# Query features halved in rows and turned by a transposing DMA

## The chip, the cores and the metric

The kernel runs on one core of a Trainium2 chip. The metric is the device time of one execution in microseconds; the time before is the median of three runs. A profiled execution has a time of its own, and a span, which runs from its first instruction to its last. TensorE is PE in the profile, VectorE DVE, ScalarE ACT, GpSimd POOL and SyncE SP; SP only issues DMAs here.

## The reference

Two independent attention blocks with 2048 tokens, 1024 features and 32 heads of 32 are computed, and their outputs stand side by side. Part A is an attention over four segments with a memory, and its output projection is the last stage of the kernel. The change is in part B:

```python
def _B_ref(x, wqkv, w_phi, wo):
    qkv = (x @ wqkv).reshape(B, S, 3, H, Dh).transpose(2, 0, 3, 1, 4)
    q, k, v = qkv[0], qkv[1], qkv[2]
    pq = einsum("bhsd,hdf->bhsf", q, w_phi)
    pk = einsum("bhsd,hdf->bhsf", k, w_phi)
    phi_q = concatenate([softmax(pq), softmax(-pq)], axis=-1)
    phi_k = concatenate([softmax(pk), softmax(-pk)], axis=-1)
    kv = einsum("bhsf,bhsd->bhfd", phi_k, v)
    z  = einsum("bhsf->bhf", phi_k)
    num = einsum("bhqf,bhfd->bhqd", phi_q, kv)
    den = einsum("bhqf,bhf->bhq", phi_q, z)[..., None] + 1e-6
    return (num / den).transpose(0, 2, 1, 3).reshape(B, S, D) @ wo
```

## The kernel before

**Numbers in two halves.** Almost every large product is done in float16, with each operand split in two float16 halves, "hi" and "lo" (lo is what hi leaves over). A product is then three matmuls: hi·hi, hi·lo and lo·hi. Making the two halves is called halving here: ACT writes hi as a copy, DVE writes lo as a subtraction.

**Stages.** Part A comes first, then the keys and values of part B, then the stage of this change, B's queries, then A's output projection. The query stage runs over 16 blocks of 128 tokens in pairs. For a pair, one Strassen product (`strassen`, L560 on: seven products of 12 matmuls of 512 columns, L584) makes the projected queries with the tokens in the rows: four tiles of 128 tokens by 512 features, that is for two blocks times two halves `hb` of 16 heads. It reads its left operand from slots that SP loads with seven DMAs of 256 KB a pair (`xkept`, L572). Each tile goes through `expo` (L1225 to L1251): two reductions and two subtractions on DVE, Exp on ACT (L1245), a sum on DVE (L1248). This gives `e`, 128 tokens by 16 heads by 2 signs by 32, float32, and `r`, the reciprocals of the softmax sums.

**The work around the change** is done for each tile (32 in all):

- POOL multiplies `e` by the key sums (L1550, two pieces), DVE sums it to `dn` (L1553, two pieces) and works out the common denominator (L1556 to L1560); L1561 multiplies it into `r`; POOL multiplies `e` by `r` (L1563). `e` is then the normalised features, 128 tokens in the rows, 1024 values each.
- TensorE turns `e` in eight float32 transposes of 128x128 (L1569) into two PSUM banks named `s`, four to a bank.
- ACT and DVE halve what stands in the banks into `pt` (L1571, L1573), with the scale 2^14, 512 values a row at a time. `pt` has the features in the rows and the tokens in the columns.
- 24 matmuls (L1582) multiply `pt` by the halved key-value sums `kls` into a bank `pv`; ACT and DVE halve that into `ot` (L1586, L1588).

When both tiles of a block are through, `project` (L1458) multiplies `ot` by the output weights (24 matmuls at L370 for each half of the columns) and SP stores the result (L1465).

**What sets the order.** The kernel is a graph of operations. Each `op(engine, duration, function, r=..., w=..., prio=...)` states what it reads and writes and a modelled duration, and a list scheduler walks the graph once by modelled times and priorities. The order in which it emits operations is the fixed order of each engine's instructions; on the chip an engine waits at its next instruction until that instruction's data are there. `lat` is the modelled time from the issue of a DMA to its landing, `kb` its size, and `port=True` marks a DVE operation on SBUF alone that the planner keeps apart from POOL's work. Buffers rotate under a tag: `e` has five slots, `pt` three, `ot` four, `os` one. An operation that writes a slot waits until the last reader of its previous contents is done.

Of the kernel before, what the change touches and what calls it, by code (L numbers as in the profile page):

```python
# [78 lines left out]
class Graph:  # L79
# [35 lines left out]
    def op(self, eng, dur, fn, r=(), w=(), prio=0, lat=0.0, short=False, port=False, need=(), kb=256):  # L115
        o = Op()
        o.short, o.port = short, port or eng == "POOL"
        o.eng, o.dur, o.fn, o.prio, o.lat, o.kb = eng, dur, fn, (prio, len(self.ops)), lat, kb
        o.banks = []
        ends, starts = set(), set()  # L120
        for b in need:
            if b.prev[0] is not None:
                ends.update(b.prev[0].ops)
        for write, accs in ((0, r), (1, w)):
            for acc in accs:
                b, key = acc if isinstance(acc, tuple) else (acc, None)
                old, last, opened = b.prev
                if old is not None:
                    ends.update(old.ops)
                if not b.ops and last is not None:  # L130
                    starts.add(last.ops[0])
                if opened is not None:
                    starts.add(opened)
                for k in (list(b.writer) if key is None else [key, None]):
                    if k in b.writer:
                        ends.add(b.writer[k])
                if write:
                    for k in (list(b.readers) if key is None else [key, None]):
# [12 lines left out]
        self.ops.append(o)  # L151
        return o
# [99 lines left out]
SP, PE, ACT, DVE, POOL = "SP", "PE", "ACT", "DVE", "POOL"  # L252
# [3 lines left out]
def tile_kernel(ctx: ExitStack, tc: tile.TileContext, ax, aw, awv, awo, beta, bx, bwqk, bwv, bphi, bwo, out):  # L256
    nc = tc.nc
# [29 lines left out]
    ident = const.tile([128, 128], F32, name="ident")  # L287
# [39 lines left out]
    for t in vfb:  # L327
        nc.gpsimd.memset(t[:, :, 128:132], 1.0)

    G = Graph(pools)  # L330
    op = G.op
# [5 lines left out]
       w=[gates], prio=0.2, lat=2.0, kb=16)  # L337
# [12 lines left out]
    def bank(tag, shape, line=None):  # L350
        b = G.bank(tag, shape, F32, line or tag)
        psums.add(b)
        return b
# [272 lines left out]
    for t in stk:  # L626
        op(ACT, 2.0, lambda t=t: nc.scalar.activation(t()[96:104, 1], sel[96:104, :, None].to_broadcast([8, 4, 512]), AF.Copy),
           w=[(t, (1, 3))], prio=0.3)
# [625 lines left out]
    def bc32(r):  # L1254
        return r()[:, :, :, None].to_broadcast([128, 16, 2, 32])

    def pairs(e):
        return e().rearrange("p (a two) s d -> p a (two s d)", two=2)

# [82 lines left out]
    for at_, p in enumerate(SEQ):  # L1342
        P = PB + 2 * at_
# [15 lines left out]
        for i in range(2):  # L1359
            if p in VT:  # L1360
                n = 2 * VT.index(p) + i
# [52 lines left out]
    P = PB + NT  # L1414
# [102 lines left out]
    for c in range(NT):  # L1517
        P = Q0 + c
        if c % 2 == 0:
            sk, er = times(c // 2, 0, P - 1.2), {}  # L1520

            def qout(i, hb, ps, er=er, sk=sk, P=P):
                er[i, hb] = expo(ps, P, sk)

            strassen(x, wqf, P - 1.2, ("proj", "proj", "proj"), CS, qout)
            if c + 2 < NT:
                x = x1 if c == 0 else xkept(c // 2 + 1, XS, P)
        ot = G.buf("b", [128, 2112], F16, "ot", 4)
        if c == 2:
            for f, i in (("B11", 8), ("B21", 13), ("T1", 12)):  # L1530
                wform[f] = G.buf("slot", [128, 2, 4, 512], F16, f"S{i}")
        if c in (1, 2, 3, 4):
            sizes_out(c - 1, P + 0.5)
        if c in (5, 7, 9, 11):
            weights((c - 5) // 2, P + 0.5)
        if c == 14:
            for i, f in enumerate(SECOND):
                wform[f] = G.buf("slot", [128, 2, 4, 512], F16, f"S{i}")
                op(SP, 0.6, lambda i=i, f=f: nc.sync.dma_start(wform[f](), wo_d[i]), r=[(wob, i)],
                   w=[(wform[f], (a, n)) for a in range(2) for n in range(4)], prio=P + 0.5, lat=1.0, kb=1024)  # L1540

        def otv(ot=ot):
            return ot()[:, 0:2048].rearrange("p (a g t) -> p a g t", a=2, g=NG)

        for hb in range(2):
            e, r = er[c % 2, hb]
            dn = G.buf("b", [128, 16, 2], F32, "dn", 2)
            for a in range(2):
                h0 = 16 * hb + 8 * a
                op(POOL, 1.35, lambda a=a, h0=h0, e=e: nc.gpsimd.tensor_tensor(  # L1550
                    e()[:, 8 * a:8 * a + 8], e()[:, 8 * a:8 * a + 8], zv()[:, h0:h0 + 8], op=OP.mult),
                   r=[zb, r], w=[(e, ("x", a))], prio=P)
                op(DVE, 0.66, lambda a=a, e=e, dn=dn: nc.vector.tensor_reduce(  # L1553
                    dn()[:, 8 * a:8 * a + 8], e()[:, 8 * a:8 * a + 8], axis=AX.X, op=OP.add), r=[(e, ("x", a))], w=[(dn, a)], prio=P)
            d1 = G.buf("b", [128, 16], F32, "d1", 2)
            op(DVE, 0.1, lambda dn=dn, r=r: nc.vector.tensor_tensor(dn(), dn(), r(), op=OP.mult),  # L1556
               r=[dn, r], w=[dn], prio=P)
            op(DVE, 0.1, lambda dn=dn, d1=d1: nc.vector.scalar_tensor_tensor(
                d1(), dn()[:, :, 0], 1e-6, dn()[:, :, 1], op0=OP.add, op1=OP.add), r=[dn], w=[d1], prio=P)
            op(DVE, 0.15, lambda d1=d1: nc.vector.reciprocal(d1(), d1()), r=[d1], w=[d1], prio=P)  # L1560
            op(DVE, 0.1, lambda d1=d1, r=r: nc.vector.tensor_tensor(  # L1561
                r(), r(), d1()[:, :, None].to_broadcast([128, 16, 2]), op=OP.mult), r=[d1, r], w=[r], prio=P)
            op(POOL, 1.95, lambda e=e, r=r: nc.gpsimd.tensor_tensor(e(), e(), bc32(r), op=OP.mult),  # L1563
               r=[e, r], w=[e], prio=P)
            pt = G.buf("b", [128, 2, 8, 128], F16, "pt", 3)
            for q in range(2):
                ps = bank("s", [128, 4, 128])
                for i in range(4):
                    op(PE, 0.11, lambda q=q, i=i, e=e, ps=ps: nc.tensor.transpose(  # L1569
                        ps()[:, i, :], pairs(e)[:, 4 * q + i, :], ident), r=[e], w=[ps], prio=P)  # L1570
                op(ACT, 0.55, lambda q=q, pt=pt, ps=ps: nc.scalar.activation(pt()[:, 0, 4 * q:4 * q + 4], ps(), AF.Copy, scale=2.0 ** 14),  # L1571
                   r=[ps], w=[(pt, (0, q))], prio=P)
                op(DVE, 0.62, lambda q=q, pt=pt, ps=ps: nc.vector.scalar_tensor_tensor(  # L1573
                    pt()[:, 1, 4 * q:4 * q + 4], ps(), 2.0 ** 14, pt()[:, 0, 4 * q:4 * q + 4], op0=OP.mult, op1=OP.subtract),
                   r=[ps, (pt, (0, q))], w=[(pt, (1, q))], prio=P)
            pn = bank("pv", [128, 4, 128])

            def f(pn=pn, pt=pt, hb=hb):
                for g in range(4):
                    for a, b in ((0, 0), (0, 1), (1, 0)):  # L1580
                        for k in range(2):
                            nc.tensor.matmul(pn()[64 * k:64 * k + 64, g, :], kls()[:, a, 8 * hb + 2 * g + k, :], pt()[:, b, 2 * g + k, :],  # L1582
                                             start=(a + b == 0), stop=(a == 1), skip_group_check=True)

            op(PE, 0.85, f, r=[(kls, (0, hb)), (kls, (1, hb)), pt], w=[pn], prio=P)
            op(ACT, 0.55, lambda pn=pn, hb=hb, otv=otv: nc.scalar.activation(  # L1586
                otv()[:, 0, 4 * hb:4 * hb + 4, :], pn(), AF.Copy, scale=2.0 ** -15), r=[pn], w=[(ot, (0, hb))], prio=P)
            op(DVE, 0.62, lambda pn=pn, hb=hb, otv=otv: nc.vector.scalar_tensor_tensor(  # L1588
                otv()[:, 1, 4 * hb:4 * hb + 4, :], pn(), 2.0 ** -15, otv()[:, 0, 4 * hb:4 * hb + 4, :], op0=OP.mult, op1=OP.subtract),
               r=[pn, (ot, (0, hb))], w=[(ot, (1, hb))], prio=P)  # L1590
        project(lambda a, g: (ot, None, lambda otv=otv: otv()[:, a, g, :]), bo, c * 128, 1024, P + 1.1)
# [116 lines left out]
```

## Time and profile before

| | |
|---|---|
| runs before, median of 3 (lowest to highest) | 1734.23 us (1733.72 to 1735.37) |
| profiled execution, its time | 1733.96 us |
| profiled execution, its span | 1732.3 us |
| granted TensorE clock, mean | 0.996 |
| ACT busy, share of the span | 1157.8 us, 67% |
| POOL busy, share of the span | 939.5 us, 54% |

The span leaves out what the profiled time has beside it, 1.7 us. A row of groups gives the line, the engine, the operation, output and inputs by name, rows by elements and type, and how often; then the busy time with the mean of one, and the idle time just ahead of them with what ended it. In a row of the timeline the first number is the start, the second the duration, and what stands in brackets is the idle time before and what ended it. A row "x24" there sums 24 instructions.

### The profile page before, as it was taken

Reading aid. Unit: us, or ns where it says so; the run is one execution under the profiler, and the core shown is the slowest. Engines: PE = TensorE matmul, PEld = TensorE weight load, DVE = VectorE, ACT = ScalarE, POOL = GpSimd, SP = SyncE. Lnnn points to the kernel's source line nnn. Section 1 sums busy time; section 2 is a strip of 40 time slices with the busy share of each in tenths; the row PEclk is TensorE's granted clock in tenths of the full one; section 3 lists DMA queues with packets and bytes.
Section 4 is the critical chain, followed back from the end, with each engine's and each line's share of the span. In section 5 each row is a group of like instructions: output and inputs, shape, how many; then the busy total and the mean of one; then the engine's idle time right before and its main releaser. Section 6 shows DMA issues by size and latency. Waiting matters only on the chain.

```text
span 1732.3 us, 39104 instructions
## 1 busy us (share of the span) xinstructions
PE 1697.2 (98%) x14664; PEld 1030.3 (59%) x14664; DVE 1384.0 (80%) x3269; ACT 1157.8 (67%) x2131; POOL 939.5 (54%) x1184
## 2 busy tenths in 40 slices
PE   8999999999999999999999999999999999999999
PEld 6667666767776676776754444444545555554444
DVE  6889899999997787889874988877978877786541
ACT  8788889888888798677772676765545544444331
POOL 3346477754478866656651777645737675440000
PEclk9999999999999999999999999999999999999999
DMA  6556455775666664743467474567413332234311
GB/s 210 160 166 185 151 169 174 223 209 169 224 181 185 188 165 122 227 162 106 136 179 262 131 240 130 180 211 251 161 44 118 103 111 85 63 139 146 122 66 63
DMA packets 194141, 273.62 MB, mean 158 GB/s; under 512 B 72224, under 2 KB 125216, under 8 KB 187424
## 3 DMA queue, kind: packets, MB, share of 16 engines
q1 hardware_dynamic: 193952, 271.13, 49.5%
q8 instruction: 115, 1.88, 0.4%
q14 instruction: 74, 0.61, 0.1%
HBM read 160.12 MB, written 85.00 MB: 142 GB/s over the span
## 4 chain that ended last, share of the span: by engine, by line
PE 40%; DVE 11%; ACT 2%; POOL 1%; issue 1%; POOLq 0%; ACTq 0%; DVEq 0%
PE proj L584 14%; PE misc L370 7%; PE proj L1636 5%; PE s L1636 2%; PE proj L370 2%; PE s L584 2%; DVE mx L1238 2%; PE misc L1636 1%; DVE r L1248 1%; PE pv L1582 1%; PE misc L584 1%; PE s L1569 1%; DVE e L1240 1%; DVE dn L1553 1%; DVE e L1242 1%; DVE pt L1389 1%
## 5 line engine op out<-in xcount | busy, mean ns | idle before, releaser
L370 PE MATMUL proj<-S,S 128*128 128x128 f16 (+1 forms) x3072 | 507.1, 300 | 4.3 <-DVE S L405 1.9
L370 PEld LDWEIGHTS <-S 128*128 128x128 f16 x4608 | 328.7, 98 | 151.2 <-issue 10.8
L584 PE MATMUL proj<-S,S 128*128 128x512 f16 x1584 | 360.6, 379 | 2.4 <-ACT cs L590 2.4
L584 PEld LDWEIGHTS <-S 128*128 128x128 f16 x2016 | 192.7, 98 | 221.7 <-issue 3.3
L960 POOL TENSOR_SCALAR_AFFINE_SELECT ph<-ph 128x256 f16<-128x256 f16 (+1 forms) x448 | 191.6, 450 | 172.5 <-DVE ph L954 133.7
L852 DVE CUSTOM_DVE_ANT_0 s<-s,causal 128x512 f32<-128x512 f32 (+3 forms) x512 | 242.6, 510 | 10.3 <-PE s L846 7.0
L954 DVE SCALAR_TENSOR_TENSOR ph<-s,ph 128x512 f16<-128x512 f32 x320 | 209.6, 683 | 51.5 <-ACT ph L953 49.3
L953 ACT ACTIVATE ph<-s 128x512 f16<-128x512 f32 x320 | 190.2, 659 | 0.3
L370 PE MATMUL misc<-S,ot 128*128 128x512 f16 x768 | 174.9, 380 | 0.0
L1245 ACT ACTIVATE e<-e,sk 128x256 f32<-128x256 f32 x256 | 113.4, 498 | 65.5 <-DVE e L1242 60.8
L370 PEld LDWEIGHTS <-ot 128*128 128x128 f16 x768 | 73.4, 98 | 81.8 <-issue 0.9
L846 PE MATMUL s<-S 96*128 96x512 f16 (+3 forms) x512 | 113.9, 299 | 2.2 <-DVE ph L954 1.6
L947 PE MATMUL s<-S 104*128 104x512 f16 (+3 forms) x512 | 113.1, 299 | 2.2 <-DVE ph L954 1.5
L951 ACT ACTIVATE s<-s,os 128x512 f32<-128x512 f32 x160 | 106.2, 717 | 6.9 <-PE s L947 5.3
L1550 POOL TENSOR_TENSOR e<-e,zb 128x512 f32<-128x512 f32 x64 | 80.2, 1277 | 55.7 <-DVE r L1248 35.1
L951 ACT ACTIVATE s<-s,bd 128x512 f32<-128x512 f32 x160 | 105.4, 705 | 6.5 <-PE s L947 6.4
L370 PE MATMUL proj<-wv,S 128*128 128x128 f16 x1536 | 101.8, 219 | 0.0
L983 PEld LDWEIGHTS <-ph 128*128 128x128 f16 x2560 | 87.3, 96 | 18.1 <-issue 2.2
L983 PE MATMUL pv<-vl,ph 128*128 128x66 f16 (+1 forms) x2560 | 91.9, 184 | 2.0 <-DVE oall L987 1.0
L1248 DVE TENSOR_REDUCE r<-e 128x32 f32<-128x1024 f32 x64 | 77.1, 1206 | 16.2 <-ACT e L1245 16.2
L1563 POOL TENSOR_TENSOR e<-e,r 128x1024 f32<-128x1024 f32 x32 | 61.9, 1938 | 34.5 <-DVE r L1561 27.5
L852 DVE DVE_READ_ACCUMULATOR2_ANT mt<- 128x1 f32 x512 | 72.6, 142 | 0.0
(344 smaller groups left out, 3344.1 us busy)
## 6 DMA issues: line engine op xcount, KB each, us to landing
S<-xf_d SPq DMA_DIRECT2D x126, 256.0 KB
S<-h SPq DMA_DIRECT2D x192, 128.0 KB
S<-wf_d SPq DMA_DIRECT2D x21, 1024.0 KB
st<-bwqk SPq DMA_DIRECT2D x64, 256.0 KB
out<-os SPq DMA_DIRECT2D x40, 256.0 KB
S<-aw SPq DMA_DIRECT2D x16, 512.0 KB
wa_d<-S SPq DMA_DIRECT2D x16, 512.0 KB
wf_d<-fo SPq DMA_DIRECT2D x32, 256.0 KB
```

The costliest lines, as they stand in the source:

```text
L370: op(PE, dur, lambda c=c, a=a, b=b, lv=lv, rv=rv: nc.tensor.matmul(pv(), lv(), rv(), start=(c == 0 and a + b == 0), stop=(c == n - 1 and a ...
L584: op(PE, 0.215, lambda n=n, a=a, b=b, lv=lv, rv=rv: nc.tensor.matmul(ps(), lv(), rv(), start=(start and n == 0 and a + b == 0), stop=(n == ...
L846: nc.tensor.matmul(ps()[:, o:o + 128 * i + 128], st()[0:96, 0, h, 128 * i:128 * i + 128], st()[0:96, 1, h, 0:128 * i + 128], start=True, s ...
L852: dve(0.12 + 0.00113 * n, lambda h=h, i=i, o=o, n=n: nc.vector.tensor_tensor_reduce(ps()[:, o:o + n], ps()[:, o:o + n], causal[:, 512 - n: ...
L947: nc.tensor.matmul(ps()[:, o:o + n], st()[0:104, 1, h, 128 * j:128 * j + 128], st()[0:104, 0, h, 128 * j:512], start=True, stop=True)
L951: act(0.59, lambda: nc.scalar.activation(ps(), ps(), AF.Exp, bias=0.0, scale=bdv()[:, 3, i2, 0:1]), r=[(bd, i2)], w=[ps])
L953: act(0.5, lambda: nc.scalar.activation(ph()[:, 0], ps(), AF.Copy, scale=2.0 ** 14), r=[ps], w=[(ph, 0)])
L954: dve(0.6, lambda: nc.vector.scalar_tensor_tensor(ph()[:, 1], ps(), 2.0 ** 14, ph()[:, 0], op0=OP.mult, op1=OP.subtract), r=[ps, (ph, 0)], ...
L960: nc.gpsimd.affine_select(pd, pd, pattern=[[0, n], [1, 128]], compare_op=OP.is_ge, fill=0.0, base=0, channel_multiplier=-1)
L983: nc.tensor.matmul(ps()[:, i, n0:n1], ph()[:, a, o:o + 128], vl()[:, j, h, n0:n1], start=(i == 0 and a == 0), stop=(j == min(i, 2)), skip_ ...
L1245: op(ACT, 0.41, lambda i=i: nc.scalar.activation(e()[:, 4 * i:4 * i + 4], e()[:, 4 * i:4 * i + 4], AF.Exp, bias=0.0, scale=sk()[:, i:i + 1 ...
L1636: op(PE, 0.215, lambda n=n, a=a, b=b: nc.tensor.matmul(ps(), v(a)[:, n, :], wform[w]()[:, b, n, :], start=(start and n == 0 and a + b == 0 ...
```

## The change

The normalised features are halved while the tokens are still in the rows, and the halves are turned by one DMA for each tile.

- The factor 2^14 moves from the halving into the multiplication of `r` (L1564 in the new numbering; below the helper `ev` all lines move down by 3, and after the edit by 7).
- For each tile a second buffer `eh` is taken from the same five slots as `e`. Read as float16 it holds 128 rows of 2 x 1024: all hi halves, then all lo halves.
- ACT writes hi (L1575) and DVE lo (L1577), 512 values a row at a time, from `e` in SBUF; before, both read PSUM.
- SP issues one transposing DMA (L1580), 128 x 2048 float16 in, `pt` as 128 x 16 x 128 out, 512 KB. The planner counts 0.6 us of issue and 2.0 us to the landing.
- The eight transposes on TensorE and their use of the banks `s` are gone. The 24 matmuls of the tile (now L1589) and what follows are unchanged.

```diff
+    def ev(e):
+        return e().rearrange("p h s d -> p (h s d)")
...
-            op(DVE, 0.1, lambda d1=d1, r=r: nc.vector.tensor_tensor(
-                r(), r(), d1()[:, :, None].to_broadcast([128, 16, 2]), op=OP.mult), ...)
+            op(DVE, 0.1, lambda d1=d1, r=r: nc.vector.scalar_tensor_tensor(
+                r(), r(), 2.0 ** 14, d1()[:, :, None].to_broadcast([128, 16, 2]), op0=OP.mult, op1=OP.mult), ...)
             op(POOL, 1.95, lambda e=e, r=r: nc.gpsimd.tensor_tensor(e(), e(), bc32(r), op=OP.mult),
                r=[e, r], w=[e], prio=P)
             pt = G.buf("b", [128, 2, 8, 128], F16, "pt", 3)
+            eh = G.buf("b", [128, 16, 2, 32], F32, "e", 5)
+
+            def hv(eh=eh):
+                return eh().rearrange("p h s d -> p (h s d)").bitcast(F16).rearrange("p (a n) -> p a n", a=2)
+
             for q in range(2):
-                ps = bank("s", [128, 4, 128])
-                for i in range(4):
-                    op(PE, 0.11, lambda ...: nc.tensor.transpose(
-                        ps()[:, i, :], pairs(e)[:, 4 * q + i, :], ident), r=[e], w=[ps], prio=P)
-                op(ACT, 0.55, lambda ...: nc.scalar.activation(pt()[:, 0, 4 * q:4 * q + 4], ps(), AF.Copy, scale=2.0 ** 14), ...)
-                op(DVE, 0.62, lambda ...: nc.vector.scalar_tensor_tensor(
-                    pt()[:, 1, 4 * q:4 * q + 4], ps(), 2.0 ** 14, pt()[:, 0, 4 * q:4 * q + 4], op0=OP.mult, op1=OP.subtract), ...)
+                op(ACT, 0.53, lambda ...: nc.scalar.activation(
+                    hv()[:, 0, 512 * q:512 * q + 512], ev(e)[:, 512 * q:512 * q + 512], AF.Copy), r=[e], w=[(eh, (0, q))], prio=P)
+                op(DVE, 0.7, lambda ...: nc.vector.tensor_tensor(
+                    hv()[:, 1, 512 * q:512 * q + 512], ev(e)[:, 512 * q:512 * q + 512], hv()[:, 0, 512 * q:512 * q + 512], op=OP.subtract),
+                   r=[e, (eh, (0, q))], w=[(eh, (1, q))], prio=P, port=True)
+            op(SP, 0.6, lambda pt=pt, hv=hv: nc.sync.dma_start_transpose(
+                pt().rearrange("p a g t -> p (a g) t"), hv().rearrange("p a n -> p (a n)")),
+               r=[(eh, (a, q)) for a in range(2) for q in range(2)], w=[pt], prio=P, lat=2.0, kb=512)
```

**The order on TensorE.** Late in the query stage, before the change, a pair's Strassen product ends (L584, `proj`), 12 transposes follow (one and a half tiles), and the next four stand three matmuls further on in the projection of an earlier block (L370, `misc`, left operand `ot`):

```order
L584 LDWEIGHTS S_14955
L584 MATMUL proj<-S_19188,S_14955 128x512
L1569 MATMUL s<-ident,e 128x128 x12
L370 LDWEIGHTS ot
L370 MATMUL misc<-S_19610,ot 128x512
L370 LDWEIGHTS ot
L370 MATMUL misc<-S_19610,ot 128x512
L370 LDWEIGHTS ot
L370 MATMUL misc<-S_19610,ot 128x512
L1569 MATMUL s<-ident,e 128x128 x4
```

After the change a product that has begun (S_13978 is one of its seven left operands) is interrupted by the first tile's matmuls, which read `pt` as the DMA left it:

```order
L584 LDWEIGHTS S_13978
L584 MATMUL proj<-S_18784,S_13978 128x512
L584 LDWEIGHTS S_13978
L584 MATMUL proj<-S_18784,S_13978 128x512
L1589 LDWEIGHTS kls
L1589 MATMUL pv<-pt,kls 64x128
L1589 LDWEIGHTS kls
L1589 MATMUL pv<-pt,kls 64x128
```

The transposes are gone, and 24 matmuls that wait for a DMA now stand inside a product, with the rest of the product and the projections behind them.

**The order on DVE,** after the change, from right behind the two pieces of a first tile's halving (L1577) to the result of its matmuls (L1595); the pieces of L1577 shown here are the second tile's:

```order
L1556 TENSOR_REDUCE dn<-e 128x16 x2
L1559 TENSOR_TENSOR dn<-dn,r 128x32
L1577 TENSOR_TENSOR e<-e 128x512 x2
L1556 TENSOR_REDUCE dn<-e 128x16
L1559 TENSOR_TENSOR dn<-dn,r 128x32
L1561 SCALAR_TENSOR_TENSOR d_22411<-dn 128x16
L1561 SCALAR_TENSOR_TENSOR d_22413<-dn 128x16
L1563 RECIPROCAL d_22411<-d_22411 128x16
L1563 RECIPROCAL d_22413<-d_22413 128x16
L1564 SCALAR_TENSOR_TENSOR r<-r,d_22411 128x32
L1564 SCALAR_TENSOR_TENSOR r<-r,d_22413 128x32
L1595 SCALAR_TENSOR_TENSOR ot<-pv,ot 128x512
```

This is all that DVE has between a tile's halving and the result that comes back through DMA, TensorE and ACT; the other two tiles' halvings stand behind L1595.

**The order on SP,** for one pair. Before, stores of the output (`os`, one slot) and loads of the next left operands follow one another:

```order
L1465 DMA out<-os 128x512 x4
L572 DMA S_13978<-xf_d 128x1024 x4
L572 DMA S_14955<-xf_d 128x1024 x3
L1465 DMA out<-os 128x512 x4
```

After, the four transposing DMAs of the pair stand between them:

```order
L1468 DMA out<-os 128x512 x2
L1580 DMA_TRANSPOSE pt<-e 128x16x128
L1468 DMA out<-os 128x512
L1580 DMA_TRANSPOSE pt<-e 128x16x128
L1468 DMA out<-os 128x512
L572 DMA S_13978<-xf_d 128x1024 x2
L1580 DMA_TRANSPOSE pt<-e 128x16x128
L572 DMA S_13978<-xf_d 128x1024
L1580 DMA_TRANSPOSE pt<-e 128x16x128
L572 DMA S_13978<-xf_d 128x1024
L572 DMA S_14955<-xf_d 128x1024 x3
```

Loads of the next product now stand behind transpositions in one queue, and a transposition waits at its place until its `eh` is written and its `pt` is free.

More of the change, by code (lines that the diff above doesn't have):

```diff
@@ L1560, in tile_kernel @@
             op(DVE, 0.15, lambda d1=d1: nc.vector.reciprocal(d1(), d1()), r=[d1], w=[d1], prio=P)
-            op(DVE, 0.1, lambda d1=d1, r=r: nc.vector.tensor_tensor(
-                r(), r(), d1()[:, :, None].to_broadcast([128, 16, 2]), op=OP.mult), r=[d1, r], w=[r], prio=P)
+            op(DVE, 0.1, lambda d1=d1, r=r: nc.vector.scalar_tensor_tensor(
+                r(), r(), 2.0 ** 14, d1()[:, :, None].to_broadcast([128, 16, 2]), op0=OP.mult, op1=OP.mult), r=[d1, r], w=[r], prio=P)
             op(POOL, 1.95, lambda e=e, r=r: nc.gpsimd.tensor_tensor(e(), e(), bc32(r), op=OP.mult),
@@ L1565, in tile_kernel @@
             pt = G.buf("b", [128, 2, 8, 128], F16, "pt", 3)
+            eh = G.buf("b", [128, 16, 2, 32], F32, "e", 5)
+            def hv(eh=eh):
+                return eh().rearrange("p h s d -> p (h s d)").bitcast(F16).rearrange("p (a n) -> p a n", a=2)
             for q in range(2):
-                ps = bank("s", [128, 4, 128])
-                for i in range(4):
-                    op(PE, 0.11, lambda q=q, i=i, e=e, ps=ps: nc.tensor.transpose(
-                        ps()[:, i, :], pairs(e)[:, 4 * q + i, :], ident), r=[e], w=[ps], prio=P)
[L1571 to L1575, printed above, removed]
+                op(ACT, 0.53, lambda q=q, e=e, hv=hv: nc.scalar.activation(
+                    hv()[:, 0, 512 * q:512 * q + 512], ev(e)[:, 512 * q:512 * q + 512], AF.Copy), r=[e], w=[(eh, (0, q))], prio=P)
+                op(DVE, 0.7, lambda q=q, e=e, hv=hv: nc.vector.tensor_tensor(
+                    hv()[:, 1, 512 * q:512 * q + 512], ev(e)[:, 512 * q:512 * q + 512], hv()[:, 0, 512 * q:512 * q + 512], op=OP.subtract),
[3 more added lines that the diff above has]
+               r=[(eh, (a, q)) for a in range(2) for q in range(2)], w=[pt], prio=P, lat=2.0, kb=512)
             pn = bank("pv", [128, 4, 128])
```

## The prediction

> **What bounds the kernel now.** I read the page's first lines, then windows over the stage that the change touches, then what TensorE waits for there.
>
> ```profile
> span 1732.3 us, 39104 instructions
> PE 1697.2 (98%) x14664; PEld 1030.3 (59%) x14664; DVE 1384.0 (80%) x3269; ACT 1157.8 (67%) x2131; POOL 939.5 (54%) x1184
> ...
> 1223.00:1265.00 42.00, 36.57 (x267) 20.46 (x264) 41.86 (x77) 20.43 (x43) 28.44 (x22) 0.96 0.36 137
> ...
> 1223.00:1583.00 360.00, 353.49 (x2397) 183.81 (x2394) 293.31 (x523) 167.18 (x323) 197.00 (x145) 1.00 0.32 108
> ...
> 1419.70:1466.10 46.40, 46.33 (x310) 23.86 (x309) 36.32 (x63) 20.40 (x41) 29.78 (x23) 1.00 0.28 86
> 1466.10:1512.40 46.30, 46.30 (x312) 23.85 (x310) 34.92 (x63) 17.73 (x36) 17.55 (x12) 1.00 0.21 63
> ...
> 1520.00:1570.00 50.00, 49.35 (x372) 26.50 (x370) 44.44 (x81) 26.02 (x50) 18.39 (x12) 1.00 0.43 155
> ```
>
> A window's columns are its length, then busy PE, weight loads, DVE, ACT, POOL, then the granted clock, the DMA share and GB/s. The query stage runs from 1223 to 1583 us. In it PE is busy 353.5 of 360 us at full clock and DVE 293.3. The two rows from 1419.7 are one pair of token blocks each: 46.3 us with PE never idle and DVE at 35 to 36. Only the head of the stage (DVE 41.86 of 42.00) and its end (DVE 44.4 of 50) are near DVE's limit. So TensorE sets the pace, and work taken from it in the steady pairs shortens the kernel for as long as the rest keeps up. Its waits in the stage say the same:
>
> ```profile
> PE pv L1582 <- DVE kls L1445: 4.0, 1, 4.0
> PE misc L1419 <- DVE za L1405: 1.3, 1, 1.3
> PE s L1569 <- POOL e L1563: 1.1, 2, 0.7
> ```
>
> **Removed from TensorE.** 32 tiles lose eight float32 transposes each.
>
> ```profile
> L1569 PE MATMUL s<-ident,e 128*128 128x128 f32 x256 | 33.6, 274 | 1.1 <-POOL e L1563 1.1
> L1571 ACT ACTIVATE pt<-s 128x512 f16<-128x512 f32 x64 | 34.6, 592 | 29.4 <-PE s L1569 29.4
> L1573 DVE SCALAR_TENSOR_TENSOR pt<-s,pt 128x512 f16<-128x512 f32 x64 | 41.0, 680 | 3.0 <-ACT pt L1571 2.8
> L1386 ACT ACTIVATE pt<-e 128x512 f16<-128x512 f32 x64 | 37.5, 620 | 27.6 <-PE kv L1396 14.3 <-POOL e L1354 12.9 <-POOL pt L1389 0.4
> L1389 DVE TENSOR_TENSOR pt<-e,pt 128x512 f16<-128x512 f32 x32 | 29.9, 948 | 4.5 <-ACT pt L1386 4.4
> L1553 DVE TENSOR_REDUCE dn<-e 128x16 f32<-128x512 f32 x64 | 42.5, 671 | 3.9 <-POOL e L1550 3.8
> ```
>
> 33.6 us busy, about 34 with the waits they stood behind, 4.2 a pair: a pair of 46.3 becomes 42.1 on TensorE. This is the most that can be won.
>
> **Exchanged on ACT and DVE.** The halving keeps its 64 + 64 instructions but reads SBUF. The nearest rows are the same two operations on the key features: ACT 620 against 592 ns, which is nothing on an engine busy 18 to 20 us of 46. On DVE the mean is 948 against 680, because POOL works beside it; undisturbed it would be the old 680. I take 948: 0.27 x 8 = 2.1 us a pair, so DVE is busy about 37.7 us (35.6 + 2.1). The factor 2^14 rides in a multiplication on 128x32 that is there in either kernel: nothing.
>
> **Added: the transposing DMA.** The trace has none. It moves 512 KB from SBUF to SBUF, and the result is wanted by the 24 matmuls of L1582. Call the time from the issue to its landing D.
>
> ```profile
> 789.45 0.55 SPq L1042 DMA_DIRECT2D wf_d<-fo  x1
> 792.63 0.63 ACT L482 ACTIVATE fo<-quad 128x512 f16<-128x512 f32 x1 [2.40 <-DMA wf_d<-fo]
> ...
> 585.83 0.51 SPq L1042 DMA_DIRECT2D wf_d<-fo  x1
> 592.94 0.63 ACT L482 ACTIVATE fo<-quad 128x512 f16<-128x512 f32 x1 [6.08 <-DMA wf_d<-fo]
> ...
> 1545.04 0.32 SPq L1601 DMA_DIRECT2D e<-oa_d  x1
> 1548.95 0.72 ACT L403 ACTIVATE h<-e,osc 128x512 f16<-128x512 f32 x1 [2.49 <-DMA e<-oa_d]
> ...
> DMA packets 194141, 273.62 MB, mean 158 GB/s; under 512 B 72224, under 2 KB 125216, under 8 KB 187424
> ...
> q1 hardware_dynamic: 193952, 271.13, 49.5%
> ```
>
> Below: an ordinary 512 KB load took 3.9 us from issue to the instruction that waited (1548.95 - 1545.04). Above: a store of 256 KB in rows of 256 bytes took 3.2 us in one place and 7.1 in another; twice the bytes at twice the longer time is 14.2. Between them: the queue's packets took 0.495 x 16 x 1732.3 / 193952 = 0.0707 us each on an engine, and 512 KB in pieces of 256 bytes are 128 on each of 16 engines: 9.05 us. I take 6.1, the middle of 3.2 and 9.05, since this transfer has the bytes of the load and presumably the row length of the store.
>
> On the Trainium skill: its page "Advanced Engine Details and Errata" (X-Bar Transpose) says that a transposing DMA on this chip is about as fast as an ordinary one. By that rule D would be near the 3.9 us of the load and the sum below would end at 1710.
>
> **What waits for it.** The new order sets all four halvings of a pair close together, and the matmuls of the first tile stand 6 to 11 matmuls into the next Strassen product. DVE meets the result of those matmuls (L1595, L1588 before) after the second halving and the small operations of two more tiles:
>
> ```profile
> 1418.29 0.86 PE L1582 MATMUL pv<-pt,kls 128*64 128x128 f16 x24
> 1419.19 0.60 ACT L1586 ACTIVATE ot<-pv 128x512 f16<-128x512 f32 x1 [2.95 <-PE pv L1582]
> ...
> 1425.19 0.69 DVE L594 TENSOR_TENSOR proj<-cs,proj 128x512 f32<-128x512 f32 x1 [4.68 <-PE proj L584]
> ...
> 1428.44 1.70 ACT L1245 ACTIVATE e<-e,sk 128x256 f32<-128x256 f32 x4
> 1430.17 1.22 DVE L1248 TENSOR_REDUCE r<-e 128x32 f32<-128x1024 f32 x1 [1.77 <-ACT e L1245]
> ...
> 1539.75 0.19 DVE L1556 TENSOR_TENSOR dn<-dn,r 128x32 f32<-128x32 f32 x1
> ...
> 1540.47 0.19 DVE L1561 TENSOR_TENSOR r<-r,d 128x32 f32<-128x32 f32 x1
> ```
>
> Between the last piece of the first halving and L1595 stand three dn sums (3 x 0.67), two halving pieces (2 x 0.95) and eight small operations (about 0.19 each): 5.4 us. The matmuls' result is there D + 0.86 + 0.60 after the issue, with some 0.4 for the three handovers: D + 1.9. DVE therefore stands still D - 3.5 in every pair, and Exp (1.8, the row at 1430.17) and the Strassen sum (I keep 1.3 of the 4.7 at 1425.19, as DVE will be the later one) hold it too. A pair lasts on DVE 37.7 + 1.8 + 1.3 + D - 3.5 = 37.3 + D, on TensorE 42.1: above D = 4.8 the wait shows. SP holds later loads behind a transposition whose `pt` is not yet free; those loads feed a product some 20 us later, so I cost that at nothing as long as D is small.
>
> **The sum,** in the profiled execution's time (1733.96; the median of the runs is 1734.23): -34.0; the head of the stage gives nothing back, because DVE is full there, and takes 2.1 for the dearer halving: +4.2 + 2.1; in the last pair DVE is the limit as well: +4.2. So far -23.5. Then 7 pairs x (6.1 - 4.8) = +9.1. Together -14.4: 1719.6, as a median 1720. In general -23.5 + 7 (D - 4.8), level at D = 8.2.
>
> **The rivals.** (a) *Latency on the other side.* The same wait with D above 8.2: at 9.05 us +6.3 (1740), at 14.2 +42.3 (1776). For it: the piece count; a store in such rows took 7.1; TensorE has no filler in front of that first product. Against it: 3.2 and 3.9 us in quiet places, and DMA shares of 0.21 to 0.28 in the steady pairs. (b) *The rate of the transposing queue.* If the four of a pair pass one after another, the queue decides once one takes more than 46.3 / 4 = 11.6 us. At 14.2 each a pair lasts 56.8, + 10.5 x 8 = +84: 1818. For it: one queue issues all four, and no row shows how fast turned pieces are written. Against it: all plain rows are faster.
>
> The Trainium skill's page "VectorE: DVE Perf Modes" (The three transpose paths) speaks for (b): it gives 1309 ns for one 128x128 block on the DMA crossbar against 390 on TensorE. No run here shows it; 16 blocks in sequence would be an estimated 21 us a transfer, 84 a pair and a time near 2030.
>
> (c) *DVE takes over without D.* DVE goes to 37.7 of 42.1 in a fixed order; if as much of its present idle time stays as 8.6 of 10.7 us, a pair keeps 46.3 and nothing changes: 1734. For it: the waits on ACT and POOL remain. Against it: its longest waits (4.7) are for TensorE and fade when that is earlier.
>
> **How the numbers follow.** Forecast with D up to 8: 0.42. Latency (a): 0.27. Rate (b): 0.18. No change (c): 0.13, of which 0.09 within 0.2% (3.5 us, about what a measurement of this kernel can tell from no change) and 0.02 on each side. Faster 0.42 + 0.02 = 0.44, same 0.09, slower 0.27 + 0.18 + 0.02 = 0.47. The likeliest single case is the forecast, 1720; its own range is 1703 (head and end give their 4.2 each and more besides) to 1731. With (a) whole and the lower part of (b) the range goes to 1800; what is left out above is most of (b).
>
> **What would show it.** L1569 gone and PE near 1663 us busy; the halving on DVE at 0.68 to 0.95 us; transpositions landing in about 6 us; pairs of 42 to 44 us; DVE's wait at L1595 of 2 to 3 us each pair, with a TensorE wait of 1 to 2 at L1589. It is wrong if a transposition takes over 8 us, if TensorE's waits for DMA in the stage exceed 34 us, or if a pair stays at 46 with D small.

## The result, and the profile after

| | median | lowest to highest |
|---|---|---|
| before, in the same runs | 1733.97 us | 1732.22 to 1735.37 |
| after the change | 1724.25 us | 1721.89 to 1726.36 |

The ratio is 0.9944, with a 95% interval of 0.9927 to 0.9961: 9.7 us faster. The forecast was 14 us, to 1720. The profiled execution took 1723.21 us, its span 1721.5, against 1733.96 and 1732.3 before. The page's first lines, and from the groups by line the rows of the new halving, of the tile's matmuls and of what follows them on DVE:

```profile
span 1721.5 us, 38668 instructions
PE 1672.6 (97%) x14408; PEld 1002.8 (58%) x14408; DVE 1403.5 (82%) x3269; ACT 1159.1 (67%) x2131; POOL 951.4 (55%) x1184
...
L1577 DVE TENSOR_TENSOR e<-e 128x512 f16<-128x512 f32 x64 | 69.5, 1124 | 7.4 <-ACT e L1575 7.3
L1575 ACT ACTIVATE e<-e 128x512 f16<-128x512 f32 x64 | 37.1, 623 | 56.2 <-POOL e L1566 43.4 <-DVE e L1577 12.7
L1589 PE MATMUL pv<-pt,kls 128*64 128x128 f16 x768 | 29.2, 228 | 21.0 <-DMA pt<-e 21.0
L1595 DVE SCALAR_TENSOR_TENSOR ot<-pv,ot 128x512 f16<-128x512 f32 x32 | 21.8, 680 | 11.6 <-ACT ot L1593 11.6
```

256 matmul instructions fewer, and TensorE busy 24.6 us less. But the span fell by 10.8 only: the tile's matmuls now wait 21.0 us for the transposing DMA, and a piece of the halving on DVE costs 1124 ns where the old one, reading PSUM, cost 680.

Windows show where that stands. Columns as in the prediction (length; busy PE, weight loads, DVE, ACT, POOL; granted clock; DMA share; GB/s); the windows are the head of the stage, the middle pairs, and its end. The kernel before, and then the changed one:

```profile
1222.00:1265.00 43.00, 37.57 (x279) 21.45 (x279) 42.86 (x79) 21.43 (x44) 28.44 (x22) 0.96 0.37 141
1265.00:1530.00 265.00, 264.57 (x1746) 135.49 (x1745) 207.25 (x367) 119.13 (x230) 152.66 (x114) 1.00 0.31 100
1530.00:1600.00 70.00, 69.35 (x464) 35.57 (x463) 55.40 (x98) 35.42 (x63) 15.90 (x10) 1.00 0.33 113
```

```profile
1222.00:1265.00 43.00, 32.64 (x220) 16.48 (x219) 42.21 (x72) 19.27 (x40) 27.45 (x21) 0.84 0.56 164
1265.00:1530.00 265.00, 258.40 (x1665) 121.86 (x1663) 237.77 (x391) 127.83 (x249) 168.78 (x119) 0.99 0.60 150
1530.00:1600.00 70.00, 65.51 (x377) 30.30 (x375) 49.83 (x83) 31.59 (x50) 10.84 (x6) 0.98 0.56 161
```

In the head TensorE lost 5 us of busy time and its clock fell from 0.96 to 0.84. In the middle it is idle for 6.6 us where it was idle for 0.4, and DVE went from 207 to 238 of 265 us: TensorE is no longer at its limit there, and DVE has little room left. The view of the chain of work that ended last says the same: over the middle, the products (L584) and projections (L370) of TensorE hold 72.0% of the time on that chain before, and 31.4% after; now DVE's lines stand on it one behind the other, with L1577 at 7.6% and the transposing DMA at 5.3%.

To split the 10.8 us, I take **the loss on TensorE**: from the end of the key stage on, the time from the start of each matmul or transpose to the start of the next, less what it takes undisturbed (the medians of the trace: 216 ns with 512 columns, 109 for a transpose, 29 for each of a tile's 24). It counts waits and the half clock (stretches with a granted clock of 0.5) together.

| loss on TensorE, us | head 1222–1265 | middle 1265–1530 | end 1530–1600 | sum |
|---|---|---|---|---|
| before | 8.3 | 5.6 | 2.0 | 15.8 |
| after | 14.6 | 13.5 | 6.9 | 34.9 |

The transposes took away 256 x 0.109 = 27.9 us, the losses gave back 34.9 - 15.8 = 19.1, and the key stage ended 2.0 us earlier in this execution (1221.1 against 1223.1; the 27 matmuls that begin 19 us into the span, which the change doesn't touch, took 6.0 instead of 7.7). 27.9 - 19.1 + 2.0 = 10.8, of which 8.8 are the change's.

**How long a transposition takes** is read from the queue of SP, TensorE's timeline and the DMA view of 1408.1 to 1410.7 us:

```profile
1406.95 2.00 SPq L1580 DMA_TRANSPOSE pt<-e  x1
...
1411.33 0.86 PE L1589 MATMUL pv<-pt,kls 128*64 128x128 f16 x24 [0.78 <-DMA pt<-e]
...
DMA packets 2062, 0.54 MB, mean 208 GB/s; under 512 B 2052, under 2 KB 2052, under 8 KB 2062
```

Issue to the waiting matmul is 4.38 us, with hardly another transfer beside it (10 larger packets). Six of the eight waiting tiles show 4.32 to 4.49; the other two, both a pair's second tile, 5.26 and 6.26. The 512 KB go as 2048 packets of 256 bytes in about 2.6 us of it; the rest is the time before the first packet and behind the last.

### The profile page after: what moved, and what is told of

It is laid out like the page before. It is cut to its first block, busy times and chain, and to the rows that moved or that the text cites. A ratio compares the mean times of both kernels' runs of the same rounds, so it can differ in the third digit from the quotient of the medians.

```text
span 1721.5 us, 38668 instructions
## 1 busy us (share of the span) xinstructions
PE 1672.6 (97%) x14408; PEld 1002.8 (58%) x14408; DVE 1403.5 (82%) x3269; ACT 1159.1 (67%) x2131; POOL 951.4 (55%) x1184
## 4 chain that ended last, share of the span: by engine, by line
PE 59%; DVE 25%; ACT 7%; POOL 3%; issue 3%; DMA 3%; DVEq 0%; ACTq 0%; SPq 0%; POOLq 0%
PE proj L370 19%; PE proj L584 11%; PE proj L1643 5%; DVE s L852 3%; PE misc L370 3%; PE s L947 3%; PE pv L983 3%; PE s L846 2%; PE s L1643 2%; DVE mx L1238 2%; DVE r L1248 2%; PE s L584 2%; DVE ph L954 2%; DVE e L1577 2%; DMA pt<-e 1%
## 5 line engine op out<-in xcount | busy, mean ns | idle before, releaser
L370 PE MATMUL proj<-S,S 128*128 128x128 f16 (+1 forms) x3072 | 506.4, 300 | 3.7 <-DVE S L405 1.3
L370 PEld LDWEIGHTS <-S 128*128 128x128 f16 x4608 | 328.7, 98 | 150.2 <-issue 9.3
L584 PE MATMUL proj<-S,S 128*128 128x512 f16 x1584 | 365.0, 381 | 2.1 <-ACT cs L590 1.9
L584 PEld LDWEIGHTS <-S 128*128 128x128 f16 x2016 | 192.8, 98 | 223.9 <-issue 8.2
L852 DVE CUSTOM_DVE_ANT_0 s<-s,causal 128x512 f32<-128x512 f32 (+3 forms) x512 | 242.4, 509 | 11.6 <-PE s L846 8.2
L370 PE MATMUL misc<-S,ot 128*128 128x512 f16 x768 | 170.5, 382 | 0.0
L370 PEld LDWEIGHTS <-ot 128*128 128x128 f16 x768 | 74.1, 98 | 89.7 <-issue 2.2
L1553 POOL TENSOR_TENSOR e<-e,zb 128x512 f32<-128x512 f32 x64 | 85.1, 1350 | 53.2 <-DVE r L1248 53.2
L370 PE MATMUL proj<-wv,S 128*128 128x128 f16 x1536 | 101.9, 219 | 0.0
L1566 POOL TENSOR_TENSOR e<-e,r 128x1024 f32<-128x1024 f32 x32 | 63.4, 1991 | 48.0 <-DVE r L1564 45.8
L1577 DVE TENSOR_TENSOR e<-e 128x512 f16<-128x512 f32 x64 | 69.5, 1124 | 7.4 <-ACT e L1575 7.3
```

Of the source, the lines that this page charges most:

```text
L370: op(PE, dur, lambda c=c, a=a, b=b, lv=lv, rv=rv: nc.tensor.matmul(pv(), lv(), rv(), start=(c == 0 and a + b == 0), stop=(c == n - 1 and a ...
L584: op(PE, 0.215, lambda n=n, a=a, b=b, lv=lv, rv=rv: nc.tensor.matmul(ps(), lv(), rv(), start=(start and n == 0 and a + b == 0), stop=(n == ...
L852: dve(0.12 + 0.00113 * n, lambda h=h, i=i, o=o, n=n: nc.vector.tensor_tensor_reduce(ps()[:, o:o + n], ps()[:, o:o + n], causal[:, 512 - n: ...
```

## The experiments

All medians stand beside runs of the kernel before on the same chip (1732.5 to 1733.3 us); the changed kernel is at 1724.25, beside 1733.97. The runs were on several chips, so a difference between two medians carries these up to 1.4 us with it, and a step of 2 to 3 us is not shown by itself.

| run | what | median us | ratio to before (95%) | loss: head, middle, end |
|---|---|---|---|---|
| e1_double | each transposition twice | 1820.52 | 1.0501 (1.0477–1.0525) | sum 132.7 |
| e2_pe_back | transposes of a constant added | 1734.52 | 1.0006 (0.9994–1.0018) | 11.9, 4.4, 1.2 |
| e3_true_durations | planner 1.15 and 2.0 us | 1729.38 | 0.9977 (0.9967–0.9988) | 14.2, 18.4, 8.8 |
| e4_ends_old | first and last pair on TensorE | 1714.54 | 0.9888 (0.9870–0.9906) | 8.3, 8.5, 1.7 |
| e5_head_old | first pair on TensorE | 1712.05 | 0.9886 (0.9869–0.9903) | 8.0, 8.0, 5.3 |
| e6_one_input | lo by an operation of one input (a probe: the remainders are left out) | 1712.67 | 0.9884 (0.9868–0.9901) | 12.3, 5.0, 4.7 |
| e7_split | two DMAs of 256 KB a tile | 1715.74 | 0.9905 (0.9888–0.9922) | 16.2, 4.9, 5.1 |
| e8_lat35 | planner: landing after 3.5 us | 1720.94 | 0.9934 (0.9919–0.9949) | 18.1, 8.1, 6.9 |
| e9_head_split | e5 and e7 | 1711.66 | 0.9879 (0.9862–0.9895) | 8.3, 6.1, 4.4 |
| e10_head_split_lat | e5, e7 and e8 | 1710.06 | 0.9872 (0.9855–0.9889) | 8.1, 7.0, 4.7 |
| e11_first_old | e5, and each pair's first tile on TensorE | 1723.14 | 0.9950 (0.9931–0.9968) | 9.4, 14.3, 3.1 |
| e12_control | planner 0.75 instead of 0.70 | 1723.45 | 0.9941 (0.9923–0.9959) | 14.2, 11.8, 8.1 |

### Does the landing time lie on the path? e1_double

```diff
+            def turn(pt=pt, hv=hv):
+                for _ in range(2):
+                    nc.sync.dma_start_transpose(pt()..., hv()...)
-            op(SP, 0.6, lambda pt=pt, hv=hv: nc.sync.dma_start_transpose(...), ...)
+            op(SP, 0.6, turn, ...)
```

> The changed kernel with each transposing DMA issued twice into the same tile, the second after the first has landed; the order is unchanged. In the changed kernel's trace a transposition that somebody waits for is there 4.3 to 4.5 us after its issue, so the time D becomes about 8.5 to 9. Theory 'latency': what is left of the loss is D, uncovered behind the first halving of a pair; each us more costs one us in each of 7 or 8 pairs: +4 x 7.5 = +30, about 1754. Rival 'DVE': the halving in rows (1.12 us a piece against 0.68) sets the pace and D is mostly covered: under +8. Rival 'rate': four issues a pair hold the queue for about 8 us each, 32 of 43: no more than 'latency' says, but loads of the next product come late.

It cost 96 us, three times what "latency" said. TensorE's waits, from the list of waits, and a pair's first tile on the queue of SP and on TensorE:

```profile
PE pv L1592 <- DMA pt<-e: 92.2, 26, 13.1
...
1346.67 6.20 SPq L1582 DMA_TRANSPOSE pt<-e  x2
...
1355.30 1.49 PE L1592 MATMUL pv<-pt,kls 128*64 128x128 f16 x24 [6.38 <-DMA pt<-e]
...
1222.00:1670.00 448.00, 352.19 (x2130) 166.54 (x2129) 306.12 (x518) 165.91 (x319) 204.19 (x145) 0.90 0.68 160
```

The landing is 8.63 us behind the first issue, 4.2 more than before. There are 26 waits now, where there were 8: not one tile of a pair, but three or four. The granted clock is 0.90 over the stage, half clock for a fifth of it: the 24 matmuls in the row take 1.49 us in place of 0.86. The doubled issue also holds SP for about 6 us a tile, and this run can't tell that from the landing. DVE is busy for 0.68 of the stage, against 0.90 in the middle of the changed kernel; "DVE sets the pace" alone is refuted for a landing of 8.6 us.

### Is TensorE still the limit? e2_pe_back

```diff
             def f(pn=pn, pt=pt, hb=hb):
+                for i in range(8):
+                    nc.tensor.transpose(pn()[:, i % 4, :], ident, ident)
                 for g in range(4):
```

> The changed kernel with eight float32 transposes of a constant put ahead of each tile's 24 matmuls, into the same bank, which the matmuls overwrite: TensorE gets its 28 us back (256 x 0.109 from start to start), all else and the order stay. Theory 'TensorE sets the pace': +20 to +28 (1744 to 1752), since only the eight tiles with a wait can hide them (0.9 us each). Rival 'DVE sets the pace': under +10.

28 us of TensorE's work cost 10.3 us, between the two theories. The row of waits shows where the rest went:

```profile
PE pv L1591 <- DMA pt<-e: 9.3, 2, 7.8
```

Outside the first pair no tile waits any more, and the loss in the middle (4.4) and at the end (1.2) is that of the kernel before or less. So with the transposes on TensorE the DMA and the dearer halving cost nothing beyond the head; without them the kernel gets 10 of 28 us, and the other 18 turn into waits and half clock. The time of this kernel is that of the kernel before (1.0006), near what it should be if the rest of the change is free outside the head, where the loss is 3.6 us above that of the kernel before.

### Is it the order? e3_true_durations, e8_lat35, e12_control

```diff
e3   -                op(DVE, 0.7, lambda q=q, e=e, hv=hv: ...
     +                op(DVE, 1.15, lambda q=q, e=e, hv=hv: ...
     -            op(SP, 0.6, lambda pt=pt, hv=hv: nc.sync.dma_start_transpose(
     +            op(SP, 2.0, lambda pt=pt, hv=hv: nc.sync.dma_start_transpose(
e8   -               ..., lat=2.0, kb=512)
     +               ..., lat=3.5, kb=512)
e12  -                op(DVE, 0.7, lambda q=q, e=e, hv=hv: ...
     +                op(DVE, 0.75, lambda q=q, e=e, hv=hv: ...
```

> The changed kernel with the planner's durations as measured: 1.15 us instead of 0.7 for a piece of the halving on DVE, 2.0 instead of 0.6 for the issue of a transposition. Theory 'order': TensorE's waits (10.9 us behind the first pair) come from an order built on halvings that end too early; they fall under 4 us and the time by 4 to 8, 1716 to 1720. Rival 'DVE sets the pace': no change within 3 us, since no order makes DVE's work less.

> The changed kernel with 3.5 instead of 2.0 us from issue to landing in the planner. Theory 'order': with 1.5 us more between halving and matmuls TensorE's waits behind the first pair fall from 10.9 to under 5: -3 to -6 (1718 to 1721). Rival 'the slots set the order, not the planner's landing': the true durations for the halving gave +5, and this gives between -2 and +6.

> The changed kernel with 0.75 instead of 0.70 us for a piece of the halving in the planner: a change with no meaning of its own that still moves instructions. It measures how far an order may move the time by itself. If the single steps of these experiments (-12.2 old head, -11.6 one input, -8.5 split, -3.3 longer landing, +5.1 true durations) are causes, this stays within 3 us of 1724; if it moves by 5 or more, the small ones (-3.3, +5.1) prove nothing.

The control moved by 0.8 us, so an order that differs without reason was worth that little in the one case tried. The durations as measured made it worse by 5.1 us, against the theory: the middle's loss rose to 18.4. The longer landing is 3.3 us faster by the medians (the middle's loss fell from 13.5 to 8.1, the head's rose by 3.5), but its interval, 0.9919 to 0.9949, overlaps the changed kernel's 0.9927 to 0.9961, so a gain is not shown. The theory "order" in the form that truer numbers in the planner mend the waits falls; that an order can cost some us stands, by e3. What in the order of e3 is worse stays open; two single waits of TensorE, 3.6 us for DVE (L1563) and 3.5 for ACT (L590), are new there.

### Where are the 18 us? e4_ends_old, e5_head_old

The edit of e4; in e5 the condition is c < 2:

```diff
+            old = c < 2 or c >= 14
...
+            for q in range(2 * old):
+                ... transposes, ACT and DVE from the banks, as before
+            if not old:
+                ... halving in rows and transposing DMA, as in the change
```

> Pairs 2 to 7 as in the changed kernel, the first and the last pair turned on TensorE as before. Theory 'the ends lose': the head of the stage lost 6.2 us to the wait and the low clock behind it and the tail 4.6, against 3.5 saved in each: -2 to -5, 1719 to 1722. Rival 'the head is late anyway, since DVE is full there': within 2 us of the changed kernel.

> Only the first pair turned on TensorE as before, pairs 2 to 8 by DMA. The kernel with both ends old took 1714.5. Theory 'the ends lose' with the head's share: after the 8.7 us wait of the changed kernel the clock stood at half for 13.7 us; both go, and 3.5 us of transposes come back: -6, about 1718; the rest of the 9.7 us is the tail's. Rival 'luck of the order': the gain of both ends came from another order of the middle pairs (their loss on TensorE fell from 12 to about 8 us there as well): within 3 us of 1724.

The first pair alone gives 12.2 us, twice what was expected; the last pair on top of it gives nothing (1714.5 against 1712.0). Why the first pair is so dear, from the changed kernel's queue and TensorE:

```profile
1244.89 13.81 SPq L1580 DMA_TRANSPOSE pt<-e  x4
...
1249.33 1.49 PE L1589 MATMUL pv<-pt,kls 128*64 128x128 f16 x24 [8.68 <-DMA pt<-e]
1252.30 1.49 PE L1589 MATMUL pv<-pt,kls 128*64 128x128 f16 x24 [1.48 <-DMA pt<-e]
1258.65 0.86 PE L1589 MATMUL pv<-pt,kls 128*64 128x128 f16 x24
```

DVE is full there, so the first transposition is issued only at 1244.89 and landed 4.4 us later, when TensorE has been out of work that stands ahead of the first tile since 1240.65. It waits 8.68 us and then runs at half clock: 43 us at 0.84 are 43 x 0.16 x 2 = 14 us at half speed, some of them in the wait. In e5 the row of the head is that of the kernel before:

```profile
1222.00:1265.00 43.00, 37.55 (x266) 21.19 (x265) 42.76 (x77) 19.79 (x42) 29.22 (x22) 0.96 0.32 122
...
PE pv L1601 <- DMA pt<-e: 4.8, 5, 2.5
```

Of the 13.6 us of loss that went, 6.6 are the head's, 5.5 the middle's, 1.6 the end's. The middle gained although nothing in it was edited. Either its pairs had inherited lateness from the head, or the planner's other order helps them: 82 and 35 matmuls stand ahead of the second pair's first two tiles in e5, 105 and 14 in the changed kernel. The runs don't tell the two apart.

### Landing or halving? e6_one_input, e7_split, e11_first_old

```diff
e6   -                op(DVE, 0.7, lambda ...: nc.vector.tensor_tensor(
     -                    hv()[:, 1, ...], ev(e)[...], hv()[:, 0, ...], op=OP.subtract),
     +                op(DVE, 0.7, lambda ...: nc.vector.tensor_reduce(
     +                    hv()[:, 1, ...], ev(e)[...].rearrange("p (n o) -> p n o", o=1), axis=AX.X, op=OP.max),
e7   -            op(SP, 0.6, lambda ...: nc.sync.dma_start_transpose(<2048 columns>), w=[pt], ..., kb=512)
     +                op(SP, 0.6, lambda ...: nc.sync.dma_start_transpose(<1024 columns of q>), w=[(pt, q)], ..., kb=256)
e11  -            old = c < 2
     +            old = c < 2 or (c % 2 == 0 and hb == 0)
```

> The changed kernel with the lo half written by a reduction over an axis of length 1, which reads e alone (in the kernel's trace reductions keep their 0.66 us with POOL beside them, the subtraction grows from 0.68 to 1.68); the lo halves are then not the remainders. Order unchanged. DVE gets 64 x (1.124 - 0.66) = 30 us free, 3.7 a pair. Theory 'DVE late': the halving ends 0.5 to 1 us earlier for a pair's first tile and all DVE work behind it earlier too; TensorE's waits behind the first pair fall from 10.9 to under 4, -6 to -10 (1714 to 1718). Theory 'latency alone': D is unchanged and the waits with it, -0 to -3.

> Each transposition in two DMAs of 256 KB, the first issued behind the first piece of the halving. Packets of a whole one took 2.45 us of the 4.4, so the second is there about 1.2 us earlier after the last piece, if the issue is not dearer. Theory 'latency': -1.2 in each of 8 waiting tiles and less time at half clock, -5 to -12 (1712 to 1719). Rival 'SP': 64 issues instead of 32 (2.2 us median each where the queue is full) hold loads and stores: 0 to +8.

> First pair on TensorE as before, and in each other pair the first tile as well; the other three tiles by DMA. In the changed kernel 6 of 8 waits of TensorE belong to the first or second tile of a pair. Theory 'latency': the waits that are left behind the first pair (4.8 us with the old head) go to under 2, and 7 x 0.9 = 6.2 us of transposes come back: +2 to +4 against 1712.0. Theory 'DVE late' gains more: 14 pieces of the halving go back to 0.68 us: -2 to +2.

Both the cheaper halving (-11.6 us, somewhat more than its theory said) and the earlier landing (-8.5) do what their theories said, and both bring the middle's loss (5.0 and 4.9) below that of the kernel before (5.6). L584 and L370 hold 72.4% of the middle's chain again in e6 and 85.9% in e7, so TensorE is back as the limit there. From the groups and waits of e6, and from those of e7:

```profile
L1577 DVE TENSOR_REDUCE e<-e 128x512 f16<-128x512 f32 x64 | 40.7, 675 | 3.0 <-POOL e L1566 2.8
...
PE pv L1589 <- DMA pt<-e: 12.1, 4, 7.6
```

```profile
L1577 DVE TENSOR_TENSOR e<-e 128x512 f16<-128x512 f32 x64 | 67.0, 1088 | 5.6 <-ACT e L1575 5.5
...
PE pv L1589 <- DMA pt<-e: 14.1, 5, 6.8
```

In e6 the halving takes 675 ns and the DMA is as slow as ever (4.46 us for the first tile), and the order on TensorE and SP is the changed kernel's, instruction by instruction; of the 10.8 us that TensorE waited for the DMA behind the first pair, 3.0 are left. In e7 the halving costs what it did (1088), and a tile's first 12 matmuls start on its first 256 KB; 2.5 us of waits are left behind the first pair. Its order on TensorE differs, though, at 253 of 14408 places, about as many as the control's 289, so e7 is the less clean of the two. So neither theory is right alone: a tile is ready when halving plus landing are through, and taking time off either one shortens the loss. In e6 all of DVE's later work comes earlier too, and the run does not part that from the halving of a waiting tile. "Latency alone", which gave e6 3 us at most, falls. e11 shows the third part of the same chain. With the first tile on TensorE there is nothing left to wait for from the DMA (1.8 us), and yet it is 11 us slower than e5: 7 x 8 x 0.109 = 6.1 us are the transposes that come back, and 26.7 - 21.3 = 5.4 are more loss.

```profile
PE s L1573 <- POOL e L1567: 5.4, 4, 2.2
...
PE pv L1601 <- DMA pt<-e: 1.8, 3, 0.7
```

The transposes now wait for POOL's multiplication ahead of them (5.4 us), and the middle's loss is 14.3. In this order a first tile's features come late from DVE and POOL already; the DMA is the last link of a late chain.

### Together: e9_head_split, e10_head_split_lat

> First pair turned on TensorE as before, the other pairs by two DMAs of 256 KB for each tile. If the two gains stand at different places (head: loss on TensorE 14.6 to 8.0 us; middle pairs: 13.5 to 8.0 with the head old alone, to 4.9 with the split alone), they add in part: middle near 5, -2 to -4 against the 1712.0 of the old head, 1708 to 1710. If the middle's loss is one of the order's luck, 1710 to 1715.

> The same with 3.5 us in the planner instead of 2.0 from issue to landing. The single change gave -3.3 on the changed kernel, of which the middle pairs' loss fell from 13.5 to 8.1. With that loss gone already by the split: within 2 us of the kernel before it in this list; if the planner's landing is an own cause, -2 to -4.

They don't add. With the head old, the split and the longer landing bring 0.4 and 2.0 us, which the runs don't tell from nothing. The losses are then 18.7 and 19.7 in all, near the 15.8 of the kernel before: of the 24.4 us of transposes in the seven turned pairs (27.9 x 28 / 32) most is now in the time. The best, 1710.06 us, has the ratio 0.9872 (0.9855 to 0.9889) to before; of its 14.2 us against the changed kernel, turning the first pair on TensorE gives 12.2 alone.

## Why the prediction was right, point by point

**The bound.** Right: TensorE set the pace, and the change won a part of what it took away. e2_pe_back shows it from the other side. The direction was held nearly even, though (slower 0.47, faster 0.44).

**Removed: 34 us, the most that can be won.** Mis-sized. The busy time counts each run of transposes until the modelled end of its last one, and the matmul behind it has started by then; from start to start they take 109 ns, 27.9 us in all. This was the row's 33.6 taken for time on the path. For this reason and the half clock PE fell to 1672.6 us busy, and not to 1663.

**ACT for nothing, DVE 0.27 us a piece.** ACT: 623 ns, right. DVE: 1124 ns, 0.44 dearer, so 3.6 us a pair instead of 2.1, and outside the 0.68 to 0.95 that was to show the forecast. The near row of the key features (948) is slowed by POOL as said, but by other work of POOL: the eight of its pieces with POOL busy all along took 1.10 us, the twenty such pieces here 1.68, and the eight of them beside POOL's multiplication of 1024 columns (L1566) 2.25.

**The landing, 6.1 us.** 4.4, near the lower bound of 3.9 that came from an ordinary load. The rule of the Trainium skill, "Advanced Engine Details and Errata" (X-Bar Transpose), that such a DMA is about as fast as an ordinary one, agrees with 4.38 against 3.9 us here. The 1309 ns that the Trainium skill's "VectorE: DVE Perf Modes" (The three transpose paths) gives for one block can't be multiplied by 16 for one DMA of 16 blocks: 2.6 us of packets are 0.16 a block.

**"DVE stands still D - 3.5 in every pair".** This step failed. DVE's waits in the stage before, and then after the change:

```profile
DVE proj L594 <- PE proj L584: 22.3, 7, 5.3
...
DVE ot L1588 <- ACT ot L1586: 11.0, 7, 2.7
...
DVE cs L594 <- PE proj L584: 6.8, 6, 2.1
```

```profile
DVE ot L1595 <- ACT ot L1593: 11.6, 7, 2.3
...
DVE cs L594 <- PE proj L584: 3.0, 2, 2.1
...
DVE proj L594 <- PE proj L584: 1.4, 2, 0.9
```

At the tile's result DVE waits as long as before, 11.6 / 7 = 1.7 us a time and not 2 to 3, and its waits for the Strassen product went, because it is the later one now. TensorE waits instead, 21.0 - 8.68 - 1.48 = 10.8 us behind the first pair. These waits are not one a pair: four first tiles wait 0.3 to 2.3 us, two second tiles 2.4 and 4.1, and pairs 2, 4 and 7 don't wait at all. With 4.4 in the forecast's own formula the pairs would have lost nothing; they lost 13.5 - 5.6 = 7.9 (forecast 9.1), because halving and landing together were late.

**The sum.** The losses were forecast at 6.3 + 4.2 + 9.1 = 19.6 us and measured at 19.1, which is luck: the halving was dearer and the landing shorter than assumed, and the losses came as waits and half clock of TensorE. The 4 us between forecast and result are the transposes, 34 against 27.9, less the 2.0 of the key stage.

**One wait a pair, 7 us for each us of D.** Wrong by a factor of three: 4.2 us more cost 96 (e1_double, with the issue on SP doubled as well), since all tiles of a pair wait then, and the clock falls. The price of rival (a) was too low, as far as a doubled issue can show it; it didn't come because the transposition was quick.

**Head and end.** The head was to lose 6.3 and lost 14.6 - 8.3 = 6.3; the end 4.2 and lost 4.9. In the head DVE was the limit, as said; the half clock behind the wait was not in the sum, so the equal number is luck as well.

**The rivals.** (b), the rate: a transposition occupies the DMA engines for about 2.6 us, four a pair are 10 of 43, so it does not decide. (c), DVE takes over: not by itself, but e6_one_input shows that 69.5 - 40.7 = 28.8 us off DVE were worth 11.6, so DVE is part of the bound now. Pairs of 42 to 44 us came, and no sign that would have refuted the forecast: between the first transpositions of pairs 2 and 8, six pairs on, lie 1537.91 - 1281.51 = 256.4 us, 42.7 each.

```profile
1281.51 1.96 SPq L1580 DMA_TRANSPOSE pt<-e  x1
...
1537.91 1.88 SPq L1580 DMA_TRANSPOSE pt<-e  x1
```

## What to carry to other kernels

Work that leaves the limiting engine is worth its time from start to start, and only as long as the data that come back over the new way are there in time: add up the whole way (producer, halving, issue, landing) and compare it with the work that stands between in the order. Where the pipeline starts, nothing stands between; leave the old way there, and change only the steady part. A TensorE that waits also can pay with half clock behind the wait: here 3.4 us after a wait of 2.39, and 13.7 around one of 8.68.

## What the runs showed of the hardware

- **Two inputs from SBUF against POOL.** Of the 64 pieces of L1577, the 26 with POOL idle took 0.68 us on the mean, the 20 with POOL busy all along 1.68. The halving from PSUM (L1573 before) took 0.68 either way, and the reduction of one SBUF input (L1556) 0.66 either way. The Trainium skill, "Advanced Engine Details and Errata" (GPSIMD Details), states such a conflict for DVE instructions with two SBUF inputs; the traces agree and add the factor of 2.5. The line's shortest, median and longest piece, in ns:

```profile
L1577 DVE TENSOR_TENSOR e<-e x64: 627/687/2403, 1242.4 to 1550.0; 128x512 f16<-128x512 f32 x64
```

- **A turned transfer lands about as soon as a plain one.** 2048 packets of 256 bytes passed in about 2.6 us, 208 GB/s, on an SBUF to SBUF transfer; 4.38 us in all, against 3.9 for the plain load of 512 KB. Its issue is dearer than that of a load: it held SP for 2.2 us at the median and up to 5.6, and 1.26 at the median for half the size; a load of 256 KB (L572) held it for 0.33 at the median.
- **The clock.** In the changed kernel half clock began 3.6 us into the wait of 8.68 us and lasted 13.7; 3.4 us of it followed each of the waits of 2.39 and 4.14, and none the wait of 2.25. "TensorE: Matmul & The Clock Gate" (What's actually happening) of the Trainium skill gives windows of about 3.4 us, idle for half clock and busy for full. The stretches, 3.4 us and four times that, agree; that a wait of 2.39 us, shorter than such a window, was enough shows that the engine need not be idle for 3.4 us in one piece.
